# Letting GpSimd's query multiply wait for VectorE's gate differences, and moving a cast and half a weight sum, in a fused attention and MLP kernel

## Chip, cores and metric

One core of one Trainium2 chip. The metric is the device time of one execution in microseconds (us). Every run that is used here is in the fast state of a one-core program. Beside the time, each run lists the mean granted clock of TensorE (1.000 is full speed).

## The reference

```python
def _attn_ref(q, k, v):                       # each (8 batches, 8 heads, 576, 64)
    q_s = exp(q - max(q, -1)); q_s = q_s / (sum(q_s, -1) + 1e-09)
    k_s = exp(k - max(k, 2));  k_s = k_s / (sum(k_s, 2) + 1e-09)
    kv = einsum('bhsd,bhse->bhde', k_s, v)
    return einsum('bhsd,bhde->bhse', q_s, kv)
def _moe_ref(x, w_in, w_out, beta):           # x = attention out as (4608, 512), d_ff 2048
    h = x @ w_in
    g = h * (1 / (1 + exp(-beta * h)))
    return g @ w_out
```

## The kernel before

The 4608 tokens are worked in nine slabs: slab t is the first 512 positions of batch t, and slab 8 holds the 8 x 64 positions left over. In a slab (slab 0, which has a plain pass 2, apart), pass 1 makes the gates GT (64 matmuls of 128x512), and pass 2 multiplies them by w_out with seven block products in Strassen's manner (112 matmuls of 128x256), for which VectorE forms sums (GS) and differences (in place in GT) of gate blocks, and sums (WSUM) of blocks of w_out; TS is its running sum of block products. The attention of the next batch is threaded between these matmuls. Its last steps are: KVD (key-value product, normalised on VectorE with RC, the reciprocals of the key sums), QT (queries normalised by a VectorE reduction and reciprocal and a multiply, then transposed by DMA), an output product KVD x QT on TensorE, and a copy to XT, which the next slab's pass 1 reads at once.

```python
def norm_main(b, hp0, n, eng=DVE):
    ...
    add(DVE, lambda e: e.tensor_reduce(s_, a, AX.X, ALU.add), r=ks, w=[("qs", i, hp0)])
    add(DVE, lambda e: e.reciprocal(v_, s_), r=[("qs", i, hp0)], w=[("qi", i, hp0)])
    add(eng, lambda e: e.tensor_tensor(a, a, vb, ALU.mult), r=ks + [("qi", i, hp0)], w=ks)
def norm_turn(b, hp0):
    norm_main(b, hp0, 2, POOL)        # multiply on GpSimd
    turn(b, hp0, 2)                   # DMA transpose EQ -> QT, issued from the Sync queue
# (cut) pass 2 of one slab
at(1); prod(z2, *gt(NG, 1), *wo(1, 0), True); ts_add(z2)
at(2)                                 # hook, slabs 1 and 2: norm_turn(next batch, head pairs 0, 1)
prod(s, GS1 ..., *wsum(0), True, True); ts_add(s)
if t > 2: g_diff(1); g_diff(0)
at(3)                                 # hook, slabs 1 and 2: norm_turn(next batch, head pairs 2, 3)
if t < 3: g_diff(1); g_diff(0)
prod(z5, *gs2(0), *wo(1, 1), False); copy(z5, 0, 1, ACTE)
# (cut) four products in all follow; the last two read the gate differences
```

In slabs 1 and 2 the first two output products of the next batch stand after 13 matmuls of the last 32 of pass 2, the other two inside the next pass 1. An engine takes its instructions in the order of the program; a helper turns declared reads and writes into semaphore waits.

The softmax here doesn't subtract the row's maximum and nothing guards it: scores larger than these inputs give would overflow.

## Time and profile before

| | before |
|---|---|
| median of 3 runs (range) | 275.59 us (275.28 to 275.67) |
| span of the profiled run | 274.1 us, clock 0.999 |
| TensorE busy | 263.8 us, 96% |
| TensorE's waits in slabs 1 and 2, by the profile | 1.48 and 1.42 us |

In the profile, PE is TensorE, DVE is VectorE, POOL is GpSimd, SPq is the Sync queue. A timeline row has start, duration, engine, source line, operation, tiles, and in brackets the idle time before it with what ended it. A row of waits has total us, count, longest. The lines of this kernel are shown in the prediction.

Some matmul records are missing from a trace, and a missing one looks like a wait. Here the first output product of slabs 1 and 2 has a weight load (74.39 in slab 1) but no matmul, and it takes 0.22 us.

### The profile page before, as it was taken

Reading aid. Unit: us, or ns where it says so; the run is one execution under the profiler, and the core shown is the slowest. Engines: PE = TensorE matmul, PEld = TensorE weight load, DVE = VectorE, ACT = ScalarE, POOL = GpSimd, SP = SyncE. Lnnn points to the kernel's source line nnn. Section 1 sums busy time; section 2 is a strip of 40 time slices with the busy share of each in tenths; the row PEclk is TensorE's granted clock in tenths of the full one; section 3 lists DMA queues with packets and bytes.
Section 4 is the critical chain, followed back from the end, with each engine's and each line's share of the span. In section 5 each row is a group of like instructions: output and inputs, shape, how many; then the busy total and the mean of one; then the engine's idle time right before and its main releaser. Section 6 shows DMA issues by size and latency. Waiting matters only on the chain.

```text
span 274.1 us, 4881 instructions
## 1 busy us (share of the span) xinstructions
PE 263.8 (96%) x1922; PEld 165.0 (60%) x1945; DVE 196.6 (72%) x415; ACT 181.0 (66%) x284; POOL 64.9 (24%) x81
## 2 busy tenths in 40 slices
PE   8999998999799998999999999999999999999995
PEld 2544444348654775468645874587448845874584
DVE  4954486787957799877878785878587639635862
ACT  4888557799178974887778937894774477018610
POOL 2790011006611078200730590036000100000000
PEclk9999999999999999999999999999999999999999
DMA  7999999999599229960289899403600030002005
GB/s 215 312 203 207 226 326 345 299 249 375 126 319 252 118 41 256 319 157 2 46 243 314 232 361 208 175 1 76 213 0 2 19 155 0 0 39 116 2 0 153
DMA packets 59367, 45.93 MB, mean 168 GB/s; under 512 B 28609, under 2 KB 58321, under 8 KB 58321
## 3 DMA queue, kind: packets, MB, share of 16 engines
q1 hardware_dynamic: 54480, 40.90, 52.5%
q0 software_dynamic: 4240, 4.19, 9.3%
q10 hardware_dynamic: 624, 0.53, 0.6%
q8 instruction: 15, 0.25, 0.4%
q14 instruction: 8, 0.06, 0.1%
HBM read 36.71 MB, written 9.44 MB: 168 GB/s over the span
## 4 chain that ended last, share of the span: by engine, by line
PE 77%; DVE 10%; DMA 8%; POOL 2%; issue 1%; SPq 0%; ACT 0%; POOLq 0%
PE PS L384 44%; PE PS L750 31%; DMA WOUT<-in_moe_w_out_dram 5%; DMA QF<-in_q_dram 3%; DVE GT L716 3%; DVE QS L338 3%; POOL WIN L574 1%; PE PS L450 1%; DVE TS L817 1%; DVE EQ L340 1%; DVE QI L339 1%; DVE WSUM L728 1%; DVE KVD L430 1%; POOL EQ L340 0%; SPq L275 0%
## 5 line engine op out<-in xcount | busy, mean ns | idle before, releaser
L384 PE MATMUL PS<-XT,WIN 128*128 128x512 bf16 x562 | 126.3, 379 | 1.2 <-issue 0.3
L650 ACT ACTIVATE GT<-PS,BETA 128x512 bf16<-128x512 f32 x144 | 95.2, 690 | 38.0 <-PE PS L384 37.6
L384 PEld LDWEIGHTS PS<-XT,WIN 128*128 128x128 bf16 x576 | 55.1, 98 | 65.1 <-DMA WIN<-in_moe_w_in_dram 0.8
L673 DVE TENSOR_SCALAR GT<-GT,RB 128x512 bf16<-128x512 bf16 x144 | 51.3, 376 | 37.9 <-ACT GT L650 37.4
L340 POOL TENSOR_TENSOR EQ<-EQ,QI 128x1024 bf16<-128x1024 bf16 (+1 forms) x13 | 25.6, 1973 | 46.9 <-DVE QI L339 46.4
L750 PE MATMUL PS<-WSUM,GT 128*128 128x256 bf16 x256 | 30.4, 273 | 2.9 <-DVE RC L458 2.9
L750 PE MATMUL PS<-WOUT,GS 128*128 128x256 bf16 x256 | 30.9, 273 | 0.1
L750 PE MATMUL PS<-WOUT,GT 128*128 128x256 bf16 x256 | 29.7, 273 | 0.0
L750 PEld LDWEIGHTS PS<-WSUM,GT 128*128 128x128 bf16 x256 | 25.0, 98 | 3.6
L750 PEld LDWEIGHTS PS<-WOUT,GS 128*128 128x128 bf16 x256 | 24.8, 98 | 3.7
L786 ACT COPY O2S<-PS 128x512 f32<-128x512 f32 (+1 forms) x17 | 9.4, 561 | 26.1 <-PE PS L750 26.0
L750 PEld LDWEIGHTS PS<-WOUT,GT 128*128 128x128 bf16 x256 | 23.9, 98 | 4.3
L355 POOL CAST VB<-VF 128x512 bf16<-128x512 f32 x25 | 17.6, 704 | 24.5 <-DVE GS L709 14.1
L307 ACT ACTIVATE EQ<-QF 128x512 bf16<-128x512 f32 x32 | 17.9, 619 | 7.8 <-DMA QF<-in_q_dram 7.7
L716 DVE TENSOR_TENSOR GT<-GT 128x2048 bf16<-128x2048 bf16 x16 | 23.1, 1483 | 0.0
L709 DVE TENSOR_TENSOR GS<-GT 128x512 bf16<-128x512 bf16 (+2 forms) x32 | 21.9, 685 | 0.0
L338 DVE TENSOR_REDUCE QS<-EQ 128x16 f32<-128x1024 bf16 (+1 forms) x20 | 19.8, 992 | 0.6 <-ACT EQ L307 0.6
L817 DVE TENSOR_TENSOR TS<-TS,PS 128x512 f32<-128x512 f32 (+1 forms) x17 | 11.0, 649 | 12.5 <-PE PS L750 10.0
L476 ACT CAST XT<-PS 128x512 bf16<-128x512 f32 x18 | 10.4, 581 | 12.1 <-PE PS L384 12.1
L307 ACT ACTIVATE EK<-KF 128x512 bf16<-128x512 f32 x32 | 18.1, 620 | 0.2 <-DMA KF<-in_k_dram 0.2
L798 DVE TENSOR_TENSOR O2S<-TS,PS 128x512 f32<-128x512 f32 (+1 forms) x17 | 10.7, 644 | 9.3 <-PE PS L750 9.3
L750 PE MATMUL PS<-WSUM,GS 128*128 128x256 bf16 x128 | 16.3, 273 | 0.2
(79 smaller groups left out, 225.2 us busy)
## 6 DMA issues: line engine op xcount, KB each, us to landing
out_dram<-O2S SPq DMA_DIRECT2D x8, 1024.0 KB, 4.9
QF<-in_q_dram SPq DMA_DIRECT2D x6, 1024.0 KB, 6.5
KF<-in_k_dram SPq DMA_DIRECT2D x6, 1024.0 KB, 9.6
VF<-in_v_dram SPq DMA_DIRECT2D x6, 1024.0 KB, 12.7
KF<-in_k_dram SPq DMA_DIRECT2D x8, 256.0 KB, 5.5
VF<-in_v_dram SPq DMA_DIRECT2D x8, 256.0 KB, 5.5
WOUT<-in_moe_w_out_dram POOLq DMA_DIRECT2D x4, 512.0 KB, 16.9
WIN<-in_moe_w_in_dram POOLq DMA_DIRECT2D x3, 512.0 KB, 9.5
```

The source lines that it names most:

```text
L307: add(ACTE, lambda e, o=o, a=a: e.activation(o, a, ACT.Exp), r=[(name + "f", i, hp)], w=[("e" + name, i, hp)])
L338: add(DVE, lambda e: e.tensor_reduce(s_, a, AX.X, ALU.add), r=ks, w=[("qs", i, hp0)])
L340: add(eng, lambda e: e.tensor_tensor(a, a, vb, ALU.mult), r=ks + [("qi", i, hp0)], w=ks)
L355: add(eng, lambda e: (e.copy if eng == ACTE else e.tensor_copy)(o, a), r=[("vf", i, hp), ("vone", i)], w=[("vb", i, hp)], after=after)
L384: add(PE, lambda e: e.matmul(o, l, r_, start=start, stop=stop), r=r, w=w, bank=[bk])
L650: add(ACTE, lambda e: e.activation(GT[:, f, :], PS[bk][:, :], ACT.Silu, scale=BETA[:, f:f + 1]), r=[("ps", bk), "beta"], w=[("gt", f, 0), ...
L673: add(DVE, lambda e: e.tensor_scalar(GT[:, f, :], GT[:, f, :], RB[:, f:f + 1], None, ALU.mult), r=k + ["rb"], w=k)
L709: add(DVE, lambda e: e.tensor_tensor(GS2[:, i:i + n, :], GT[:, i:i + n, :], GT[:, i + NG:i + NG + n, :], ALU.add), r=[k_ for f in (i, i + ...
L716: add(DVE, lambda e: e.tensor_tensor(gv(f, th, NG), gv(f, 1 - th, NG), gv(f, th, NG), ALU.subtract), r=gk(f, 0, NG) + gk(f, 1, NG), w=gk(f ...
L750: add(PE, lambda e, l=l, r_=r_, st=st, u=u, i=i, b_=b_: e.matmul(PS[b_][:, 256 * u:256 * u + 256], l, r_, start=st, stop=end and i == NG - ...
L798: add(DVE, lambda e, b_=b_, u0=u0, u1=u1: e.tensor_tensor(o[:, u0:u1, :], ts[:, u0:u1, :], bank3(b_)[:, u0:u1, :], ALU.subtract), r=["ts", ...
L817: add(DVE, lambda e, b_=b_, c=c: e.tensor_tensor(TS[:, c], TS[:, c], PS[b_][:, c], ALU.add), r=["ts", ("ps", b_)], w=["ts"], bank=[b_])
```

## The change

The intent: GpSimd's multiplies and VectorE's gate differences got in each other's way in slabs 1 and 2, and KVD, behind the differences on VectorE, came late. So the differences go ahead of the second reduction, GpSimd's first multiply waits for them, and the first two output products move 6 matmuls later. At the end of slab 0, batch 1's first value cast goes from GpSimd to VectorE, and half of one w sum moves into slab 1.

```diff
-        def norm_main(b, hp0, n, eng=DVE):
+        def norm_main(b, hp0, n, eng=DVE, sums=True, mult=True, after=()):
     ...                      # reduction and reciprocal if sums, multiply (with after=) if mult
+        def mult_turn(b, hp0):
+            norm_main(b, hp0, 2, POOL, sums=False, after=P.writer[("gt", 0, 1)])
+            turn(b, hp0, 2)
     ...                      # slabs 1 and 2, output products of the next batch
-                return s + spread(x[0:2], 117, 120)
+                return s + spread(x[0:2], 120, 123)
     ...                      # pass 2
             ts_add(s)
-            if t > 2:
-                g_diff(1)
-                g_diff(0)
+            g_diff(1)
+            g_diff(0)
             at(3)
-            if t < 3:
-                g_diff(1)
-                g_diff(0)
     ...                      # slab 0
-                todo += [(x, one(cast_v, 1, hp, DVE if hp else POOL)) ...
+                todo += [(x, one(cast_v, 1, hp, DVE)) for hp, x in ((1, 118.5), (2, 123), (3, 127))]
     ...
-                norm_main(1, 3, 1, DVE)
+                norm_main(1, 3, 1, DVE, mult=False)
+                cast_v(1, 0, DVE)
+                norm_main(1, 3, 1, DVE, sums=False)
                 w_sum(0, 4, 4)
-                w_sum(2, 4, 4)
     ...                      # slab 1
-                             (6.1, one(w_diff, 0)), (6.2, one(w_diff, 1))]
+                             (6.1, one(w_sum, 2, 4, 4)), (6.2, one(w_diff, 0)), (6.3, one(w_diff, 1))]
     ...                      # hooks of slab 1 (batch 2); slab 2 the same with batch 3
-                on(2, norm_turn, 2, 0)
+                on(2, norm_main, 2, 0, 2, POOL, True, False)
+                on(3, mult_turn, 2, 0)
                 on(3, norm_turn, 2, 2)
```

## The prediction

> **What bounds the kernel now.** I read the page first (busy shares, then the costliest groups), then the chain of work that ended last, then the waits of TensorE, and only then timelines of single engines in the two places that the change touches.
>
> ```profile
> span 274.1 us, 4881 instructions
> PE 263.8 (96%) x1922; PEld 165.0 (60%) x1945; DVE 196.6 (72%) x415; ACT 181.0 (66%) x284; POOL 64.9 (24%) x81
> PEclk9999999999999999999999999999999999999999
> ...
> L716 DVE TENSOR_TENSOR GT<-GT 128x2048 bf16<-128x2048 bf16 x16 | 23.1, 1483 | 0.0
> ```
>
> TensorE is busy 96% of the span at full clock, so everything that scheduling can give is in its roughly 10 us of idle time. The waits of TensorE say where a change of this kind can reach:
>
> ```profile
> PE PS L750 <- DVE RC L458: 2.9, 2, 1.5
> PE PS L384 <- DVE WARM L226: 1.2, 1, 1.2
> PE PS L384 <- POOL VB L355: 0.5, 1, 0.5
> ...
> PE PS L384 <- DVE KVD L430: 0.3, 1, 0.3
> ```
>
> The first row is two waits of 1.5 us, one in slab 1 and one in slab 2. The third and fourth are in the tail of slab 0. These are the targets of the two halves of the change. In slab 1 the chain of waits (start, duration) runs through VectorE:
>
> ```profile
> 67.51 0.55 DVE TS L817
> 68.05 1.13 DVE QS L338
> 69.19 0.02 issue
> 69.21 0.25 DVE QI L339
> 69.47 4.35 DVE GT L716 x2
> 73.81 0.09 DVE RC L458
> 73.91 0.03 issue
> 73.93 0.61 DVE KVD L430 x2
> ...
> 74.64 0.49 PE PS L750 x3
> ```
>
> The two gate differences (L716) take 4.35 us here; the reader should set this beside slab 3, where they take 2.35 us with GpSimd idle. In slab 1 GpSimd is running its query norm multiplies at that very time (timelines of VectorE in slab 3, GpSimd and the DMA queue in slab 1):
>
> ```profile
> 126.35 2.35 DVE L716 TENSOR_TENSOR GT<-GT 128x2048 bf16<-128x2048 bf16 x2
> ...
> 67.99 4.74 POOL L340 TENSOR_TENSOR EQ<-EQ,QI 128x1024 bf16<-128x1024 bf16 x2
> ...
> 69.92 4.07 SPq L503 DMA_TRANSPOSE QT<-EQ  x2
> ```
>
> TensorE's attention output product of head pair 0 needs two things: KVD (end of the VectorE chain) and QT, the transposed normalised queries (GpSimd multiply, then DMA transpose). The weight load of that product starts at 74.39. KVD of pair 0 is done at 73.93 + 0.35 = 74.28. The first transpose starts at 69.92 and lands 3.1 us later, at 73.0 (the view of the transpose line: "DMA to landing us min/median/max: 3.1/3.1/3.1" for that one). So KVD is last today, but QT leads it by only 1.3 us. In slab 2 the same figures are 103.52 for the load, 103.41 for KVD, and 99.05 + 3.1 = 102.15 for QT.
>
> **What the Trainium skill says.** "SBUF — State Buffer", section "SBUF: two separate sides": GpSimd and VectorE share a port pair that is an exclusive lock; a VectorE operation with two SBUF inputs and a GpSimd operation that reads SBUF exclude each other, and the loser waits. The trace agrees in direction: alone a gate difference takes 1.22 us and a GpSimd multiply 1.90 us, and in slab 1 the overlapped pair takes 2.92 and 2.76 us. "VectorE: DVE Perf Modes", section "The perf-mode tier table", gives 1224 ns for a bf16 tensor-tensor of 2048 elements; the undisturbed ones here measure 1220, so 1.22 is the floor for them. The same table has the reduction at 1x only; it takes 1.21 us here whether GpSimd multiplies beside it or not. "DMA: Bandwidth & Descriptors", section "DMA Transpose (X-bar)", says such a transpose is issued from the Sync or Scalar queue but states no time to landing for a small SBUF one; the 3.1 us of the trace is used.
>
> **The change, part by part: slabs 1 and 2.** The order of instructions shows on VectorE: last TS add, both gate differences, then the second reduction and reciprocal, then the KVD chain. GpSimd's first multiply now waits for the second difference. On TensorE the first two output products move 6 matmuls later (13 before it become 19).
>
> Slab 1, in the times of the old trace. The TS add ends at 67.43 + 0.63 = 68.06. The differences, undisturbed, run from 67.98 (starts overlap ends by 0.08, as in slab 3) to 67.98 + 2.35 = 70.33. The reduction and reciprocal add 1.4, RC and KVD of pair 0 about 0.5: KVD is ready at about 72.2, 2.1 us earlier than 74.28. This is the gain that is meant.
> But QT moves the other way. GpSimd starts 0.15 after a VectorE result (as at 106.99 to 107.14): 70.33 + 0.15 = 70.48. Plus 1.90: 72.38. The transpose follows 0.03 later, at 72.41, and lands at 75.51; with 0.08 for the semaphore TensorE can go on at about 75.6. Without a stall it would want the product after 19 matmuls from 71.58, at 71.58 + 19 x 0.109 = 73.65. So it waits about 1.9 us, now for the transpose. Against the old start at 74.39 the product is 1.2 us later, but 6 more matmuls (6 x 0.109 = 0.65) are already done: slab 1 loses 1.2 - 0.65 = 0.55 us.
> Slab 2: the TS add ends at 96.89 + 0.63 = 97.52, the differences at 99.79, multiply 99.94 to 101.84, transpose 101.87 to 104.97, TensorE at 105.05 against 103.52 before. It loses 1.53 - 0.65 = 0.9 us. Here GpSimd had started right behind its reciprocal (97.12), while in slab 1 its casts had already delayed it, so the added wait is larger.
> The second multiply ends 2.0 us after the first, its transpose lands about 2.0 us after the first, at 77.5; its product comes 1.87 + 0.22 = 2.1 us after the first one, so it just fits. Sum for this half: +1.4 us.
>
> **Tail of slab 0.** Today the value cast of pair 0 runs on GpSimd and ends TensorE's wait:
>
> ```profile
> 41.14 1.00 POOL L355 CAST VB<-VF 128x512 bf16<-128x512 f32 x1 [0.56 <-DMA VF<-in_v_dram]
> ...
> 40.98 0.69 DVE L340 TENSOR_TENSOR EQ<-EQ,QI 128x512 bf16<-128x512 bf16 x1
> 41.59 1.70 DVE L728 TENSOR_TENSOR WSUM<-WOUT 128x1024 bf16<-128x1024 bf16 x2
> 43.21 0.15 DVE L458 RECIPROCAL RC<-PS 128x1 f32<-128x1 f32 x1
> ```
>
> On VectorE it takes 0.42 and can start when the data land, 41.14: done at 41.56, so the KV product can start at 41.62 instead of 42.20. The query multiply follows at 41.49 to 42.18, one w sum (0.69) ends at 42.79, and RC starts at about 42.7 instead of 43.21, because only half of the two w sums stands before it. Everything after is a cycle of RC, KVD, product, cast of about 1.54 us per pair, and moves forward by 0.5; the remaining value and key blocks land early enough (the next one at 42.5, wanted at 43.2). The moved w sum (0.6 to 0.7) then delays the gate scaling on VectorE at about 52, where VectorE has waits of 0.2 to 0.7 for ScalarE and TensorE waits for none of it: free. Sum: -0.5 us.
>
> Total: 275.6 + 1.4 - 0.5 = 276.5 us.
>
> **The rivals.** (1) The gain arrives as meant: QT is not last. For it: the gate differences surely go from 4.35 to 2.35, and the whole 1.48 and 1.42 of TensorE idle would vanish, with 0.5 from slab 0: about 272.2 us. Against it: it needs QT by 73.7, and the multiply starts only at about 70.5; multiply plus transpose are 5.0 us. No timeline leaves room for that.
> (2) As I have it, the wait changes its name from KVD to the transpose: 276.5.
> (3) The second transposes, or the XT copies behind them, are late as well; the margin of 0.1 us is thin, and each miss would add a few tenths per slab: up to 277.3.
> (4) Slab 0 gives nothing, since VectorE idles for the data and the next blocks are on their way: the whole would be 277.0. Against it is that the data wait is only 0.2 us.
> For all of them, contention of later GpSimd casts (about 1.7 us later in slab 2) with the gate scaling costs VectorE a little, off TensorE's path.
>
> **Range and chances.** I give (2) with its neighbours (3) and (4) about 80% and (1), wholly or in part, 20%. I take 276.3 as the point, a little below 276.5 for the share of (1), and 274.0 to 277.2 as the range for 8 in 10. Two per cent would be 5.5 us: more than all the waits that are touched, and more than the losses that I can sum. Faster by over 2%: 0.02; within 2%: 0.97; slower: 0.01.
>
> **What would show it.** Right: L716 falls to about 1.22 us for all 16, so its mean from 1483 to about 1230; the multiply starts at about 70 in slab 1 behind L716; the transposes land after KVD, and TensorE's idle before the output product is 1.8 to 2.1 us in slabs 1 and 2, released by the transpose and no longer by VectorE; slab 1's first gate product starts about 0.5 us earlier than before. Wrong: no idle there over 0.5 us, or the multiply below 1.5 us, or a transpose landing in much less than 3 us; then (1) holds and the time is 272 to 273.

## The result

The changed kernel took 277.08 us (median of 6, 276.62 to 277.79) against 275.62 us of the kernel before in the same rounds (median of 6, 275.16 to 275.74). The ratio is 1.0058, 95% interval 1.0043 to 1.0073: slower by about 1.5 us. A ratio here is always the mean time of one kernel's fast runs over that of the other's in the same rounds, so it is not quite the ratio of the medians.

The time lies inside the stated range, but the loss was forecast at 0.7 us (276.3 for 275.6) and measured at 1.5.

From the page of the changed kernel:

```profile
span 275.2 us, 4906 instructions
PE 265.3 (96%) x1945; PEld 164.3 (60%) x1945; DVE 194.1 (71%) x416; ACT 180.8 (66%) x284; POOL 61.4 (22%) x80
...
L723 DVE TENSOR_TENSOR GT<-GT 128x2048 bf16<-128x2048 bf16 x16 | 19.7, 1272 | 0.0
```

The gate differences (now L723) did fall, from 1483 to 1272 ns on average, and VectorE is less busy. The waits of TensorE show where that went:

```profile
PE PS L387 <- DMA QT<-EQ: 3.9, 3, 1.8
PE PS L387 <- DVE WARM L226: 1.2, 1, 1.2
```

Two waits for VectorE (1.5 us each by the profile, 1.2 to 1.3 without the missing records) have become three waits, 3.9 us in sum, for the DMA transpose. The chain of waits through slab 1 (start, duration), and its piece at the end of slab 2:

```profile
67.18 2.27 DVE GT L723 x2
69.46 0.02 issue
69.48 0.02 POOLq L139
69.50 0.10 issue
69.60 1.91 POOL EQ L343
71.51 0.01 issue
71.52 3.15 DMA QT<-EQ
74.67 0.05 issue
74.72 0.39 PE PS L387
...
101.56 1.91 POOL EQ L343
103.47 0.02 issue
103.48 3.79 DMA QT<-EQ
107.28 0.05 issue
107.33 2.76 PE PS L387 x12
```

Differences, multiply, transpose, product: these now stand one behind the other. In slab 2 the second transpose is last as well, and it took 3.79 us to land.

The time can be followed at fixed points of the timelines of the two traces (of TensorE, but for the first row):

| point | before | after | shift | added by the part just passed |
|---|---|---|---|---|
| VectorE's first w sum, ahead of all that was changed | 30.06 | 29.72 | -0.34 | (chance) |
| first matmul of slab 1's pass 2 | 61.71 | 60.84 | -0.87 | end of slab 0: -0.53 |
| first matmul of slab 2's pass 1 | 76.93 | 76.58 | -0.35 | slab 1: +0.52 |
| first matmul of slab 3's pass 1 | 106.06 | 106.51 | +0.45 | slab 2, first product: +0.80 |
| third output product of slab 2 | 106.27 | 107.33 | +1.06 | slab 2, second transpose: +0.61 |
| end of span | 274.1 | 275.2 | +1.1 | nothing |

Without the chance of the first row that is -0.53 + 0.52 + 0.80 + 0.61 = +1.40 us, which agrees with the timed difference of medians, 1.46. (The third product is the first that needs the second transpose.)

### The profile page after: what moved, and what is told of

It reads as the page before. It is cut to its first block, busy times and chain, and to the rows that moved or that the text cites. A ratio compares the mean times of both kernels' runs of the same rounds, so it can differ in the third digit from the quotient of the medians.

```text
span 275.2 us, 4906 instructions
## 1 busy us (share of the span) xinstructions
PE 265.3 (96%) x1945; PEld 164.3 (60%) x1945; DVE 194.1 (71%) x416; ACT 180.8 (66%) x284; POOL 61.4 (22%) x80
## 4 chain that ended last, share of the span: by engine, by line
PE 82%; DVE 8%; DMA 5%; SPq 2%; POOL 1%; issue 1%; ACT 0%; POOLq 0%
PE PS L387 51%; PE PS L757 30%; DMA QT<-EQ 3%; DMA VF<-in_v_dram 2%; DVE QS L339 2%; DVE GT L723 2%; POOL EQ L343 1%; PE PS L453 1%; DVE TS L824 1%; SPq L287 1%; SPq L275 1%; DVE EQ L343 1%; DVE QI L341 1%; DVE VB L358 0%; DVE KVD L433 0%
## 5 line engine op out<-in xcount | busy, mean ns | idle before, releaser
L387 PE MATMUL PS<-XT,WIN 128*128 128x512 bf16 x576 | 128.2, 379 | 0.1
L343 POOL TENSOR_TENSOR EQ<-EQ,QI 128x1024 bf16<-128x1024 bf16 (+1 forms) x13 | 23.9, 1835 | 53.1 <-DVE QI L341 33.7
L358 POOL CAST VB<-VF 128x512 bf16<-128x512 f32 x24 | 16.5, 689 | 22.3 <-DVE GS L716 13.6
L723 DVE TENSOR_TENSOR GT<-GT 128x2048 bf16<-128x2048 bf16 x16 | 19.7, 1272 | 0.0
```

Source lines behind the costliest of these rows:

```text
L358: add(eng, lambda e: (e.copy if eng == ACTE else e.tensor_copy)(o, a), r=[("vf", i, hp), ("vone", i)], w=[("vb", i, hp)], after=after)
L387: add(PE, lambda e: e.matmul(o, l, r_, start=start, stop=stop), r=r, w=w, bank=[bk])
L723: add(DVE, lambda e: e.tensor_tensor(gv(f, th, NG), gv(f, 1 - th, NG), gv(f, th, NG), ALU.subtract), r=gk(f, 0, NG) + gk(f, 1, NG), w=gk(f ...
```

## The experiments

Twelve runs were made of eleven kernels (one was run twice), in five rounds beside the kernel before. All gave right results.

| run | ratio to before (95%) | median us | runs with a clock of 0.994 or less |
|---|---|---|---|
| the change | 1.0058 (1.0043 to 1.0073) | 277.08 | 1 of 6 |
| slab 0 part alone | 0.9987 (0.9975 to 0.9999) | 275.13 | 0 of 5 |
| slabs 1 and 2 alone | 1.0078 (1.0055 to 1.0100) | 277.14 | 2 of 6 |
| before, products later | 1.0025 (1.0013 to 1.0037) | 276.15 | 0 of 5 |
| the same, reduction moved | 0.9972 (0.9959 to 0.9984) | 274.68 | 0 of 5 |
| change, products earlier | 1.0130 (1.0099 to 1.0160) | 279.23 | 4 of 6 |
| the same again | 1.0144 (1.0121 to 1.0167) | 279.35 | 5 of 6 |
| the same, wait filled | 1.0080 (1.0067 to 1.0093) | 277.78 | 0 of 4 |
| change, load behind transpose | 1.0077 (1.0060 to 1.0095) | 277.41 | 3 of 6 |
| change, wait for one difference | 1.0040 (1.0028 to 1.0052) | 276.56 | 0 of 5 |
| change, no wait | 1.0192 (1.0154 to 1.0230) | 280.57 | 4 of 6 |
| second multiply on VectorE | 0.9936 (0.9924 to 0.9948) | 273.76 | 0 of 5 |
| multiply between differences | 0.9917 (0.9905 to 0.9929) | 273.04 | 0 of 5 |

My theory at the start: the whole loss is TensorE waiting for the transposed queries. The rivals were that the later place of the products does the harm, and that part of the loss comes from slab 0.

### The two halves apart

Slab 0's edits alone (the cast and the w sum of the diff above):

> The kernel before with the slab 0 part of the change alone. Theory (the loss is all in slabs 1 and 2, where TensorE's wait moved from KVD to the transposed queries): TensorE starts slab 1's second pass about 0.5 us earlier, ratio to before 0.998 (275.1 us). Rival (the two parts disturb each other, or slab 0 itself gives nothing): ratio 1.000 or above.

Measured: 0.9987, that is 0.4 us faster; the interval reaches from nothing to 0.7 us. The trace starts slab 1's pass 2 at 60.69 us; that of the whole change starts it at 60.84.

The change without them:

> The change without its slab 0 part. Theory: the losses of 0.52 us (slab 1), 0.80 us and 0.61 us (slab 2, first and second product) stay whole, so about 1.9 to 2.0 us over before, ratio 1.007; the gate differences take 2.35 us a pair and the first product waits 1.7 to 1.8 us for the transpose in both slabs. Rival (part of the loss comes from the extra VectorE work at the turn from slab 0 to 1): ratio 1.005 or less.

Measured: 1.0078. Its trace has two waits for the transpose of 3.5 us in sum in place of the change's three, and its second transpose in slab 2 landed in 3.4 us. So the first half pays a little and the second costs all of the loss. The rival that put part of the loss on slab 0 fell.

### The place of the products

The same one line of edit, once into the kernel before and, reversed, into the changed one:

```diff
-                return s + spread(x[0:2], 117, 120)
+                return s + spread(x[0:2], 120, 123)
```

> The kernel before, with only the first two output products of slabs 1 and 2 moved 6 matmuls later. Theory: KVD still comes at the same time, but 6 more matmuls of 0.109 us are done before the wait, so each slab gains about 0.65 us: ratio 0.995 (274.3 us), TensorE's wait 0.8 us a slab instead of 1.5. Rival (the later place of the products itself costs, as the copies to XT come too late for the next slab's first pass): ratio 1.001 or more.

Measured: 1.0025, slower. Here my theory missed and the rival was right in direction. The trace tells why. VectorE and TensorE in slab 2 of this run (timelines):

```profile
104.14 1.21 DVE L338 TENSOR_REDUCE QS<-EQ 128x16 f32<-128x1024 bf16 x1
105.38 0.25 DVE L339 RECIPROCAL QI<-QS 128x16 f32<-128x16 f32 x1
105.55 0.63 DVE L476 CAST XT<-PS 128x512 bf16<-128x512 f32 x1
...
106.24 0.39 PE L384 MATMUL PS<-XT,WIN 128*128 128x512 bf16 x1 [1.43 <-DVE XT L476]
```

The wait of 1.2 to 1.3 us did shrink, to 0.5 and 0.4 us. What is left of it stands ahead of the seventh block product, which reads the second gate difference: the difference ends at 73.46 in slab 1 and TensorE goes on at 73.61. (The view of waits names RC, which runs at the same time.) But being later in the program, the XT copy of the first product fell behind batch 4's reduction in VectorE's order, and the next pass 1 waited 1.4 us for it. In slab 1, where no reduction stands there, 0.4 us of gain was kept (5.35 us from the last 32 matmuls' start to the next pass 1 became 4.94).

So the next run moved only that reduction (with its multiply) into slab 3, behind the XT copies:

```diff
-                on(6, norm_turn, 4, 0)
-                    todo += [(4, one(norm_turn, 4, 2))]
+                    todo += [(3.9, one(norm_turn, 4, 0)), (4, one(norm_turn, 4, 2))]
```

> The kernel before with later products, and batch 4's first reduction and multiply moved behind the XT copies of slab 2. The later products alone cost 0.25%, not the gain of 0.5% that was expected; in their trace TensorE waits 1.4 us in slab 2 for an XT copy that stands behind that reduction on VectorE. Theory: that order was all that hid the gain, so the wait goes and the ratio is 0.995 to 0.996. Rival (the later place costs by itself): ratio 1.000 or more, with a wait for XT in slab 1 too.

Measured: 0.9972, 0.8 us faster than before and 1.5 us faster than without the move. The wait of 1.4 us for XT is gone. The view still has four waits, 1.3 us in sum: in each slab one of 0.4 to 0.5 before the seventh block product, which ends 0.14 after the second gate difference, and one of 0.2 where the record of the first output product is missing. So with the products later it is no longer KVD that comes last but the slowed second difference, which does not move: the gain was 0.8 of the 1.3 us that were expected.

> The change, with the products put back to their old place (13 matmuls ahead instead of 19). Theory: the transpose lands at the same time, the wait grows by 6 x 0.109 us in each of the two slabs, so 1.3 us over the change: ratio to before 1.0105, waits of about 2.4 us. Rival (the later place of the products is what costs): faster than the change, ratio 1.004 or less.

Measured: 1.013. The waits for the transpose grew to 2.7 and 2.4 us, as expected of a transpose that lands at its own time. The rival (the products' place is the harm in the changed kernel) fell: there the reduction is over at 104.2, before the first product of slab 2 at 104.65, so it holds up no XT copy. But the time came out 2.2 us above the change, by medians, for 1.3 us expected, and the runs were far apart: two at clock 1.000 took 277.5 us, four at 0.988 to 0.994 took 279.2 to 280.7. The two at full clock are only 0.5 us above the change at full clock (276.99): their trace has the longer waits, but not the third wait of slab 2.

### The clock

> The same kernel as the change with its products put back, once more, as the control of the next run on one chip. In its first timing two of six runs had a granted clock of 1.000 (277.5 us), four had 0.988 to 0.994 (279.2 to 280.7 us). Theory (TensorE's idle of 2.4 to 2.7 us sometimes lowers its clock for a while): again several runs at 0.994 or less and about 279 us. Rival (that chip or hour was uneven): all runs at 0.997 or more and 277.5 us.

Measured: 1.0144; one run at clock 1.000 (278.33 us), five at 0.988 to 0.994 (279.15 to 281.04). This time the profiled run was one of the low ones. Stretches of its trace around the two waits (columns: stretch, length, busy time of PE, PEld, DVE, ACT and POOL with instructions, granted clock, DMA share, GB/s):

```profile
70.00:75.00 5.00, 2.35 (x22) 1.98 (x22) 2.12 (x8) 0.59 (x1) 3.37 (x2) 1.00 0.35 71
75.00:77.00 2.00, 2.00 (x14) 1.47 (x14) 1.28 (x2) 0.58 (x1) 0.00 (x0) 0.73 0.96 179
77.00:80.00 3.00, 3.00 (x14) 1.62 (x13) 0.69 (x1) 0.50 (x1) 0.00 (x0) 0.61 0.98 329
80.00:84.00 4.00, 4.00 (x20) 1.81 (x19) 2.08 (x4) 3.71 (x7) 1.07 (x2) 1.00 1.09 354
```

In the first stretch TensorE stands idle for 2.65 us (2.4 without a product whose record is missing); in the next two the clock is 0.73 and 0.61; then it is full again. The same goes with the wait of slab 2. The clock that is missing is (1 - 0.73) x 2 + (1 - 0.61) x 3 = 1.7 us; were it half speed, it would have lasted 3.4 us. Finer stretches of the trace show just that: the clock is 0.50 from 75.90 to 79.31 and from 106.62 to 110.03. That is the window and the half rate that the Trainium skill gives in "TensorE: Matmul & The Clock Gate", section "Part 1: The HAM clock gate": an idle window of about 3.4 us drops the array to half clock. By that page (section "Why this matters for your kernels") a gap under 3 us should be harmless; here, in a kernel whose two traces have gaps of 2.4 to 2.7 us, the clock was low in 9 of 12 runs.

Why not in all? In these traces the clock changes only at whole multiples of 3.41 us from its first change. Before each of the three falls in the traces (these two, and one of "no wait" at 78.48) TensorE had stood idle for 2.2 to 2.3 of the 3.41 us. The earlier trace of this same kernel kept full clock with gaps of 2.4 and 2.7 us, but there they lay across two such stretches, at most 1.7 us in one; and no other trace has more than 1.8 us of idle in such a stretch of slabs 1 and 2. So where a wait falls in these stretches seems to decide; three falls are few, and it was not tested.

To test that the idle is the cause, matmuls on zeros were put into the wait:

```diff
-                return s + spread(x[0:2], 117, 120)
+                return s + [(116.99, lambda: warm(10, HB[(hrot[0] + 1) % 3]))] + spread(x[0:2], 117, 120)
```

> The same, but ten idle matmuls of 128x512 on zeros (10 x 0.217 = 2.2 us, into a bank that nobody uses then) stand before the first product of slabs 1 and 2, so TensorE works while it waits for the transpose. Theory of the clock: every run at 0.997 or more, all near 277.5 us, ratio to before 1.007, although it does more work. Rival (the low clock has nothing to do with the idle): as many runs at 0.994 or less as the control, ratio 1.012 to 1.013.

Measured: 1.0080; all four runs at a clock of 0.999 or more, 277.44 to 277.90 us, where 9 of 12 runs without the filling had a low one. A kernel that does 20 more matmuls is 1.6 us faster by medians than its control on the same chip. Its timeline in slab 1 (one of the ten records is missing):

```profile
71.84 2.11 PE L387 MATMUL PS<-WARM 128*128 128x512 bf16 x9
74.23 0.39 PE L387 MATMUL PS<-QT,KVD 128*128 128x512 bf16 x1 [0.28 <-DMA QT<-EQ]
```

So a long wait of TensorE costs twice in some runs: once as itself, and about 1.7 us again as a low clock after it. In the changed kernel this is small: one of its six runs (0.993) took 277.79 us, the other five 276.99 on average.

### The second transpose of slab 2

```diff
-                on(3, load, 5)
+                on(3, lambda: load(5, after=P.writer[("qt", 1, 2)]))   # handed on to the qf load
```

> The change, with the query load of batch 5 (slab 2) waiting until the second transpose has landed. In the change's trace that transpose landed in 3.8 us instead of 3.1, and the second product waited for it. Theory (the load's packets on the same engines delay it): 3.1 to 3.2 us again, no wait of over 0.1 us before that product, ratio to before 1.003 to 1.004 instead of 1.006. Rival (something else, such as the 8 KB instruction fetch seen on one engine at that moment): still over 3.4 us, ratio unchanged.

Measured: the transpose still took 3.7 us to land and TensorE still waited 0.4 us; ratio 1.0077, at full clock 276.99 us (mean of three), the same as the change. The theory of the load fell. What remains is the rival: in the seven traces where this transpose landed in 3.7 us or more, the packets show an 8 KB instruction fetch of 0.31 us on one DMA engine just ahead of the transpose's last completion writes; in the traces of before, of slabs 1 and 2 alone and of the best kernel there is none there, and it landed in 3.1 to 3.4. (In before and in slabs 1 and 2 alone there is one earlier, 1.1 and 1.5 us after the issue and not 2.5 or more.) That is a coincidence in time and no test, and 0.31 us is only half of the delay. The cause stays open.

### The wait itself

```diff
-            norm_main(b, hp0, 2, POOL, sums=False, after=P.writer[("gt", 0, 1)])
+            norm_main(b, hp0, 2, POOL, sums=False, after=P.writer[("gt", NG, 0)])
```

> The change, but GpSimd's first multiply waits for the first of the two gate differences only. Theory (exclusive port, and the second difference starts at once and holds it): the multiply is drawn out to about 3 us and ends no more than 0.15 us earlier, ratio 1.005 to 1.006. Rival (the two share): the multiply ends about 1 us earlier, TensorE's wait shrinks to below 1 us, ratio 1.000 or below.

The view of the multiply's line, slab 1 of this run, and then slab 1 of the change:

```profile
L343 POOL TENSOR_TENSOR EQ<-EQ,QI x1: 2742/2742/2742, 68.4 to 68.4; 128x1024 bf16<-128x1024 bf16 x1
```

```profile
L343 POOL TENSOR_TENSOR EQ<-EQ,QI x1: 1898/1898/1898, 69.6 to 69.6; 128x1024 bf16<-128x1024 bf16 x1
```

Counted from the end of the differences, which differs by 0.05 us between the two traces, the multiply starts 1.14 us earlier and lasts 0.84 us longer: it stands behind the second difference, which keeps its 1.2 us. It ends 0.3 us earlier, more than the 0.15 I allowed; why is not shown. The ratio is 1.0040, a little under the 1.005 to 1.006 that was forecast and far from the rival's 1.000. The lock theory holds.

No wait at all, everything else as in the change:

```diff
-                on(2, norm_main, 2, 0, 2, POOL, True, False)
-                on(3, mult_turn, 2, 0)
+                on(2, norm_turn, 2, 0)          # the same for batch 3
```

> The change without GpSimd's wait: the first multiply starts as soon as its reciprocal is there, while the differences still stand ahead of the second reduction. Theory: the first transpose is in time, but the second multiply now comes after slowed differences and its transpose 2.5 us too late for the second product: TensorE waits there in both slabs, ratio 1.008 to 1.012, slower than the change. Rival (the added wait is the whole loss): ratio 0.995 or below.

Measured: 1.0192, the slowest of all. In slab 1:

```profile
66.72 4.05 DVE L723 TENSOR_TENSOR GT<-GT 128x2048 bf16<-128x2048 bf16 x2
...
66.74 2.95 POOL L343 TENSOR_TENSOR EQ<-EQ,QI 128x1024 bf16<-128x1024 bf16 x1
72.34 1.90 POOL L343 TENSOR_TENSOR EQ<-EQ,QI 128x1024 bf16<-128x1024 bf16 x1 [2.65 <-DVE RC L461]
...
77.45 0.39 PE L387 MATMUL PS<-QT,KVD 128*128 128x512 bf16 x1 [2.23 <-DMA QT<-EQ]
```

With the differences ahead of the second reduction, the second multiply starts only at 72.3, and TensorE waits 2.2 us for its transpose (1.7 in slab 2, after 1.4 for the XT copy behind the reduction). At full clock the two runs took 279.2 us on average, ratio 1.0135; the other four had a low clock. So once the differences go first, the wait is no longer the worst of it: the order on VectorE is. "The added wait is the whole loss" fell.

### A kernel that beats both

What the runs ask for: both multiplies early, differences undisturbed, XT copies not behind a reduction. On GpSimd the two multiplies take 4.7 us beside the differences (kernel before), so the second goes to VectorE:

```diff
# slab 0 as in the change; slabs 1 and 2 (shown for batch 2), products at 120
-                on(2, norm_main, 2, 0, 2, POOL, True, False)
-                on(3, mult_turn, 2, 0)
-                on(3, norm_turn, 2, 2)
+                on(2, norm_turn, 2, 0)               # first multiply at once on GpSimd
+                on(3, norm_turn, 2, 2, DVE)          # second on VectorE, then the differences
# batch 4's casts on GpSimd wait for the differences; batch 4's first reduction in slab 3
```

> Candidate: the slab 0 part kept; in slabs 1 and 2 the first multiply runs at once on GpSimd, the second on VectorE ahead of the gate differences (about 1.2 us more of VectorE), batch 4's casts wait for the differences, and batch 4's first reduction goes behind the XT copies. Theory: both transposes land before KVD, the differences run undisturbed after 70.6, KVD is ready at about 73.4 to 73.9, just when TensorE comes to the product: waits of 0.3 us or less, ratio 0.988 to 0.991 (272.3 to 273.1 us). Rival (VectorE is now the bound, as it has the extra multiply): waits of 1 us or more for KVD, ratio 0.997 or above.

Measured: 0.9936, no wait for KVD or QT, but TensorE waits 0.5 us in each slab for the first gate difference, which I had not looked at: the sixth block product needs it. So the last run puts that difference ahead of the multiply:

```diff
# (cut) pass 2, slabs 1 and 2; the hook with the second norm_turn goes
+                norm_main(t + 1, 2, 2, DVE, mult=False)
                 g_diff(1)
+                norm_main(t + 1, 2, 2, DVE, sums=False)
+                turn(t + 1, 2, 2)
                 g_diff(0)
```

> The candidate with the second multiply on VectorE, ratio 0.9936, whose trace shows TensorE waiting 0.5 us a slab for the first gate difference. Here that difference goes ahead of the multiply. Theory: the two waits of 0.5 us go, nothing else becomes last (the second transpose has over 1 us in hand), ratio 0.990. Rival (in slab 1 the difference meets GpSimd's multiply and loses what it gained; KVD stays last): ratio 0.993 or above.

Measured: 0.9917, 273.04 us (273.00 to 273.67), 2.3 us faster than before (0.4 of it is the slab 0 part) and about 4 us faster than the change; the 0.990 that was forecast was just missed. The view has one wait left in the two slabs, of 0.2 us, and there the record of the first output product is missing again, so it is none. (Some 0.3 us in slab 2, in pieces too short for the view, go to a ScalarE copy of a block product.)

```profile
68.06 1.59 DVE L723 TENSOR_TENSOR GT<-GT 128x2048 bf16<-128x2048 bf16 x1
69.58 1.21 DVE L343 TENSOR_TENSOR EQ<-EQ,QI 128x1024 bf16<-128x1024 bf16 x1
70.71 1.21 DVE L723 TENSOR_TENSOR GT<-GT 128x2048 bf16<-128x2048 bf16 x1
...
72.75 0.38 PE L757 MATMUL PS<-WSUM,GT 128*128 128x256 bf16 x2 [0.19 <-DVE RC L461]
```

The first difference still meets GpSimd's multiply in slab 1 (1.59 for 1.21), and that is what is left of the disturbance there.

## Why the prediction was right or wrong

- **What bounds the kernel, and the step of slab 0.** Right. -0.5 was predicted, -0.53 is in the trace, and 0.4 was timed for that half alone.
- **The gate differences fall to their floor and KVD comes 2 us earlier.** Right: 2.35 us a pair in both slabs, and KVD of the first pair done at 71.3 in slab 1, 3.4 us before TensorE's product.
- **The transpose takes KVD's place.** Right to a tenth: in the frame of the old trace the product was to start at 75.6 in slab 1, and it started at 74.72 + 0.87 = 75.59. +0.55 and +0.9 were predicted, +0.52 and +0.80 measured. This was the prediction's own choice among its rivals, and rival (1) was plainly false.
- **"Its product comes 1.87 + 0.22 = 2.1 us after the first one, so it just fits."** This step failed. It held in slab 1. In slab 2 the second transpose took 3.8 us instead of 3.1, and TensorE lost 0.61 us. The term was put at 0 in the sum. Rival (3) named it, as a few tenths. Why the landing was late is open (the load is ruled out, the instruction fetch is untested).
- **The point.** The prediction's own sum was 276.5; with 0.61 more and slab 2's 0.1 less it would have been 277.0, beside 277.08. I then took 276.3 "for the share of (1)", a rival that no timeline supported. Of the 0.8 us between forecast and measured loss, this is 0.2 and the late second transpose 0.6. (The 272.2 us of rival (1) were too low by 0.4 besides: the 1.48 and 1.42 us in it hold two missing records of 0.22. The sum for (2) goes by weight loads and is not touched.)
- **Not foreseen at all.** That a wait of TensorE can lower its clock afterwards. For the change itself it is worth little (one run of six), for its neighbours with longer waits it is 1.7 us, or twice that.
- **Also not foreseen.** The 6 later matmuls were counted as free work before the wait. The run with the later products alone shows that this holds only while something else hides the XT copy that moves with them.

## What to carry to other kernels

When an engine is made to wait so that another runs faster, follow what the waiting engine feeds: here 2.1 us gained on VectorE were paid with 2.5 us (slab 1) on a chain of multiply and transpose that had only 1.3 us in hand. Moving an instruction later also moves what follows it in the program on the other engines, and in-order queues make that a new wait. Where a wait of the matmul engine of some 2 us and more can't be avoided, look at the granted clock of every run, and try filling it with idle matmuls. Before reading a small wait of TensorE, look whether every weight load has its matmul.

## What the Trainium skill lacked or had wrong

- "TensorE: Matmul & The Clock Gate": it asks for gaps under about 3 us. In a kernel with waits of 2.4 to 2.7 us the mean clock was 0.988 to 0.994 in 9 of 12 runs, with waits of up to 2.2 us in 4 of 6 (no wait), and with waits of 1.7 to 1.8 us still in 6 of 18 (the change, slabs 1 and 2 alone, load behind transpose). In the traces 2.2 to 2.3 us of idle in a stretch of 3.41 us came before each fall. That about 3.4 us at half clock follow agrees with the page.
- "DMA: Bandwidth & Descriptors": in the section on the DMA transpose, no time to landing for one of 128x1024 bf16 from SBUF to SBUF (the skill has a time only for a single 128x128 block). In slabs 1 and 2 of the kernel before it was 3.1 to 3.2 us; the second one of slab 2 took 3.7 to 4.0 where an 8 KB instruction fetch fell into its end (cause not proven). Beside the three loads of 1 MB the next one took 9.2.
- "SBUF — State Buffer": nothing wrong, but no durations for such a pair. Its exclusive lock is borne out (a multiply of 1.90 us behind a difference lasts 2.74; a pair of differences that meets it takes 4.05 for 2.35). So is the order of issue: in the kernel before, the second multiply, issued at 69.97 and waiting, went ahead of VectorE's next difference, issued at 70.89, and they took 2.76 and 2.92 us.
